# Attention decode block on one Trainium2 core: V as the moving operand, one V tile and wo loaded in parts, c and x as rows, the store from ACT

## The chip, the cores and the metric

The kernel runs on one core of one Trainium2 chip. The metric is device microseconds of one execution, as a median of several. Every experiment ran beside the kernel before on the same chip. A "ratio" is the mean time of one kernel's fast runs over that of the other's of the same rounds, so it is not quite the ratio of the medians that are quoted beside it. Profiles show one execution; its span is some 2 us shorter than the measured time (358.2 us beside 360.28 us for the kernel before).

## The reference, cut to what matters

One token goes through an adaptive-layernorm block: attention against a cache, then a small ReLU network. Everything is bf16.

```python
mod = (silu(c) @ w_mod)                     # six vectors of 512
h = layernorm(x) * (1 + ca) + sa
q = h @ wq                                  # 32 query heads of 128
# 8 kv heads, 4 query heads each, 32768 keys of 128: K and V are 64 MB each (2**20 bytes)
o = softmax(q k^T / sqrt(128)) v
x = x + ga * (o @ wo)                       # wo: 4096 x 512
h = layernorm(x) * (1 + cb) + sb
x = x + gb * (relu(h @ w1) @ w2)            # 512 -> 1792 -> 512
```

Nearly all of the 149.4 MB that must be read are K and V, and each is used once. The kernel is a stream of loads with computation beside it.

## The kernel before

All weights and tiles go through one ring of eight slots of 2 MB, in one order, from SP's queue. A tile of K or V is 128 partitions of 64 rows of 128 values: 16 KB per partition.

```python
stream = [("wm", 0), ("wm", 1), ("wq", 0), ("wq", 1)]
stream += [("k", 0, u) for u in range(NTILE)]
for g in range(Hkv):
    if g == Hkv - 1:
        stream.append(("wo", 0))
    for u in range(NTILE):
        if g + 1 < Hkv:
            stream.append(("k", g + 1, u))
        stream.append(("v", g, u))
stream += [("wo", 1), ("w1",)] + [("w2", i) for i in range(len(W2P))]
# in load(key): one transfer per tile
        i = nc.sync.dma_start(out=t[:], in_=src)

def pv(g, u):                               # V tile as weights, probabilities move: 64 small matmuls
    # ... cut
    for j in range(TK):
        c0 = (16 * G + j % 16) * 32 + REP * (s0 + j // 16)
        nc.tensor.matmul(oT_ps[:], lhsT=Vsb[:, j, :], rhs=PT_g[:, c0:c0 + REP],
                         start=(u == 0 and j == 0), stop=(u == NTILE - 1 and j == TK - 1))

# the end: wo's second half lands last of the attention weights, then w1, then w2 in three parts
project(1)                                  # 64 matmuls
# ... residual, layernorm, 56 matmuls with w1, relu
x1_rows = rows4(x1T[:], "x1_rows")          # 16 matmuls of one column: x1 as four rows
# ... 56 matmuls with w2 into ffn_ps, then two vector operations
nc.sync.dma_start(out=..., in_=o_bf...)     # the result
```

`c` and `x` are loaded by ACT's queue as 128 columns, in pieces of 8 bytes.

## Time and profile before

| kernel before | value |
|---|---|
| time, median of 3 runs | 360.28 us (359.99 to 360.31) |
| span of the profiled run | 358.2 us |
| mean granted TensorE clock | 0.77 |

The page's part 1 (busy time of each engine and its share of the span), part 2 (the span in 40 slices: TensorE clock, DMA share in tenths, GB/s), parts 3 and 4 (DMA queues with packets, MB and share; the chain of waits by engine), and from part 5 the group of matmuls with V:

```profile
PE 237.5 (66%) x3138; PEld 136.9 (38%) x3138; DVE 184.5 (52%) x207; ACT 27.0 (8%) x65; POOL 8.3 (2%) x13
...
PEclk9999996986597659876698659686968869665555
DMA  7999999999999999999999999999999999999993
GB/s 302 428 434 423 430 437 432 417 435 432 434 421 437 428 426 432 434 424 432 434 429 424 432 429 435 426 426 432 428 435 427 423 435 434 426 426 435 426 413 119
...
q8 instruction: 24, 0.39, 0.4%
q10 hardware_dynamic: 288, 0.00, 0.0%
...
DMA 77%; DVE 11%; PE 10%; issue 1%; ACT 0%; DVEq 0%
...
L374 PE MATMUL oT_ps<-PT_g,Vsb 128*128 128x4 bf16 x2048 | 56.6, 164 | 9.5 <-DMA Vsb<-in_A_v_cache_dram 5.1
```

The DMA engines are full in all slices but the first and the last, at about 430 GB/s. No compute engine is near its limit (PE, the busiest, is at 66%). 149.4 MB at 430 GB/s are 347 us, so the span can only shrink by a leaner stream or by shorter ends. The chain of waits agrees: 77% of it is DMA. Queue q8 holds the instruction fetches: 24 packets and 0.39 MB for PE's 6090 instructions. They move on the same engines as the data (section 9: after the first of them one of the sixteen landings of a transfer comes about 1.3 us behind the rest).

The tail, from the timeline (start, duration, engine, line, operation, count, and in brackets the idle time before it with its releaser):

```profile
345.75 2.29 PE L407 MATMUL attnT_ps<-o_sb,wo_sb 128*128 128x1 bf16 x64 [2.29 <-DMA wo_sb<-in_A_wo_dram]
...
350.58 1.63 PE L450 MATMUL hidT_ps<-h2T,w_sb 128*128 128x1 bf16 x56 [1.28 <-DVE h2T L207]
...
352.14 1.00 PE L240 MATMUL x_rows_ps<-ident_f,x1T 128*1 128x32 f32 x29
...
353.07 1.78 PE L465 MATMUL ffn_ps<-w_sb,hidT 128*1 128x128 bf16 x50
...
354.48 0.10 PEld L465 LDWEIGHTS <-hidT 128*1 128x1 bf16 x7 [0.19 <-issue]
354.91 0.29 DVE L471 TENSOR_TENSOR o_rows<-ffn_ps,gb_rows_sb 128x128 f32<-128x128 f32 x1 [1.28 <-PE ffn_ps L465]
...
355.56 0.66 SPq L474 DMA_DIRECT2D out_dram<-o_bf  x1
```

The last wo part lands at 345.7 us. Its matmuls take 2.3 us, then come a layernorm, the hidden layer (350.58), x1_rows (352.14) and the matmuls with w2, until 354.9. The last weight loads of w2, at 354.48, come just as the last part of w2 lands (issued at 330.9, 23.6 us to landing). So the compute chain and the stream end nearly together.

### The profile page before, as it was taken

How to read it: one execution, taken by the hardware profiler on the slowest of the kernel's cores; microseconds unless marked ns; L12 is line 12 of the kernel's file. 1: busy time of each engine (PE TensorE's matmuls, PEld its weight loads, DVE VectorE, ACT ScalarE, POOL GpSimd, SP SyncE). 2: the span in 40 equal slices, each digit the busy share in tenths (PEclk: the TensorE clock that was granted, in tenths of full speed). 3: DMA queues.
4: the chain of work that ended last, by engine and by line, in shares of the span. 5: the costliest groups of instructions: out<-in, count | busy, mean ns of one | idle time of the engine just before them, and what ended most of it. 6: DMA issues, size and time to landing. Idle time of an engine off the chain costs nothing.

```text
span 358.2 us, 6817 instructions
## 1 busy us (share of the span) xinstructions
PE 237.5 (66%) x3138; PEld 136.9 (38%) x3138; DVE 184.5 (52%) x207; ACT 27.0 (8%) x65; POOL 8.3 (2%) x13
## 2 busy tenths in 40 slices
PE   0547775857587839755777758883956576895454
PEld 0543333433254425423343425341523334445354
DVE  4419976552954465553954385456655394342012
ACT  1111022002000110002000200011000100003000
POOL 9000000000000000000000000000000000000000
PEclk9999996986597659876698659686968869665555
DMA  7999999999999999999999999999999999999993
GB/s 302 428 434 423 430 437 432 417 435 432 434 421 437 428 426 432 434 424 432 434 429 424 432 429 435 426 426 432 428 435 427 423 435 434 426 426 435 426 413 119
DMA packets 11492, 149.86 MB, mean 418 GB/s; under 512 B 1480, under 2 KB 1480, under 8 KB 2376
## 3 DMA queue, kind: packets, MB, share of 16 engines
q1 hardware_dynamic: 11176, 149.43, 98.0%
q8 instruction: 24, 0.39, 0.4%
q10 hardware_dynamic: 288, 0.00, 0.0%
q14 instruction: 4, 0.03, 0.0%
HBM read 149.42 MB, written 0.00 MB: 417 GB/s over the span
## 4 chain that ended last, share of the span: by engine, by line
DMA 77%; DVE 11%; PE 10%; issue 1%; ACT 0%; DVEq 0%
DMA Ksb<-in_A_k_cache_dram 67%; DVE KTt L309 9%; DMA wo_sb<-in_A_wo_dram 9%; PE S_ps L318 6%; PE oT_ps L374 1%; DMA xc_bf<-in_c_dram 1%; PE attnT_ps L407 1%; PE ffn_ps L465 0%; PE hidT_ps L450 0%; ACT P_g L351 0%; DVE PT_g L356 0%; PE x_rows_ps L240 0%; DVE S_g L324 0%; PE stat_ps_ln L189 0%; PE L_ps L361 0%
## 5 line engine op out<-in xcount | busy, mean ns | idle before, releaser
L318 PE MATMUL S_ps<-KTt,qbd 128*128 128x512 bf16 x512 | 159.1, 475 | 59.8 <-DVE KTt L309 58.9
L309 DVE STREAM_TRANSPOSE KTt<-Ksb 128x2048 f32<-128x2048 f32 x64 | 143.7, 2286 | 47.6 <-DMA Ksb<-in_A_k_cache_dram 47.6
L318 PEld LDWEIGHTS <-qbd 128*128 128x128 bf16 x512 | 59.3, 117 | 148.5 <-issue 117.8
L374 PE MATMUL oT_ps<-PT_g,Vsb 128*128 128x4 bf16 x2048 | 56.6, 164 | 9.5 <-DMA Vsb<-in_A_v_cache_dram 5.1
L374 PEld LDWEIGHTS <-Vsb 128*128 128x128 bf16 x2048 | 56.3, 97 | 16.8 <-DMA Vsb<-in_A_v_cache_dram 5.4
L324 DVE TENSOR_SCALAR_CACHE_REDUCE S_g<-S_ps 128x512 f32<-128x512 f32 x16 | 11.0, 687 | 50.8 <-PE S_ps L318 50.8
L289 ACT COPY qbd<-qrep_sb 32x128 bf16<-32x128 bf16 x32 | 9.4, 295 | 187.0 <-PE S_ps L318 185.8
L356 DVE STREAM_TRANSPOSE PT_g<-P_g 128x1024 bf16<-128x1024 bf16 x8 | 10.0, 1245 | 17.5 <-ACT P_g L351 17.5
L361 PE MATMUL L_ps<-Lexp,ones_f 128*128 128x4 f32 x16 | 4.5, 351 | 21.1 <-DVE Lexp L359 21.1
L361 PEld LDWEIGHTS L_ps<-Lexp,ones_f 128*128 128x128 f32 x16 | 4.0, 311 | 21.5 <-issue 21.5
L383 DVE TENSOR_TENSOR oT_sb<-oT_ps,Linv 128x4 bf16<-128x4 f32 x8 | 1.3, 162 | 20.4 <-PE oT_ps L374 20.4
L226 PE MATMUL modT_ps<-siluT,wm_sb 128*128 128x1 bf16 x96 | 3.5, 172 | 10.8 <-DVE siluT L218 10.6
L351 ACT ACTIVATE P_g<-S_g,nbias 128x1024 bf16<-128x1024 f32 x8 | 9.2, 1147 | 0.2
L348 ACT ACTIVATE nbias<-Mb_ps 128x1 f32<-128x1 f32 x8 | 1.4, 172 | 90.2 <-PE Mb_ps L346 90.2
L226 PEld LDWEIGHTS <-wm_sb 128*128 128x128 bf16 x96 | 3.4, 118 | 10.8 <-DMA wm_sb<-in_w_mod_dram 7.5
L267 PE MATMUL qT_ps<-hT,wq_sb 128*128 128x1 bf16 x128 | 3.7, 165 | 5.2 <-DVE hT L207 2.7
L346 PE MATMUL Mb_ps<-ident_f,Mexp 1*128 1x1 f32 x16 | 3.5, 284 | 5.5 <-DVE Mexp L341 5.5
L407 PE MATMUL attnT_ps<-o_sb,wo_sb 128*128 128x1 bf16 x128 | 4.6, 172 | 2.3 <-DMA wo_sb<-in_A_wo_dram 2.3
L174 DVE CAST cT<-xc_bf 128x4 f32<-128x4 bf16 x1 | 3.8, 3764 | 4.2 <-DMA xc_bf<-in_c_dram 4.2
L346 PEld LDWEIGHTS Mb_ps<-ident_f,Mexp 1*128 1x128 f32 x16 | 2.8, 217 | 7.4 <-DVE Mexp L341 7.0
L267 PEld LDWEIGHTS <-wq_sb 128*128 128x128 bf16 x128 | 3.6, 104 | 5.3 <-issue 2.8
L407 PEld LDWEIGHTS <-wo_sb 128*128 128x128 bf16 x128 | 4.6, 119 | 2.4 <-DMA wo_sb<-in_A_wo_dram 2.4
(83 smaller groups left out, 53.5 us busy)
## 6 DMA issues: line engine op xcount, KB each, us to landing
Ksb<-in_A_k_cache_dram SPq DMA_DIRECT2D x32, 2048.0 KB, 34.0
Vsb<-in_A_v_cache_dram SPq DMA_DIRECT2D x32, 2048.0 KB, 34.5
wq_sb<-in_A_wq_dram SPq DMA_DIRECT2D x2, 2048.0 KB, 19.6
wo_sb<-in_A_wo_dram SPq DMA_DIRECT2D x2, 2048.0 KB, 31.9
wm_sb<-in_w_mod_dram SPq DMA_DIRECT2D x2, 1536.0 KB, 8.1
w_sb<-in_B_w_dram SPq DMA_DIRECT2D x1, 1792.0 KB, 33.8
w_sb<-in_B_w_dram SPq DMA_DIRECT2D x1, 1024.0 KB, 30.4
w_sb<-in_B_w_dram SPq DMA_DIRECT2D x1, 512.0 KB, 24.6
```

The costliest lines, as they stand in the source:

```text
L226: nc.tensor.matmul(modT_ps[:, j * KT + ko:j * KT + ko + 1], lhsT=lhsT[:, ko, :], rhs=siluT[:, kt:kt + 1], start=(kt == 0), stop=(kt == KT ...
L267: nc.tensor.matmul(qT_ps[:, hq:hq + 1], lhsT=wq_sb[kt // 2][:, kt % 2, hq * Dh:(hq + 1) * Dh], rhs=hT[:, kt:kt + 1], start=(kt == 0), stop ...
L289: nc.scalar.copy(out=o, in_=i)
L309: nc.vector.transpose(out=KTt[:].bitcast(F32), in_=Ksb[:, 32 * half:32 * half + 32, :].rearrange("p j d -> p (j d)").bitcast(F32),)
L318: nc.tensor.matmul(S_ps[:], lhsT=qbd[g % 2][:, hp, s, :], rhs=KTv[:, 16 * sl:16 * sl + 16, h, :, par], start=(t4 == 0 and sl == 0 and hp = ...
L324: nc.vector.tensor_scalar(out=S_tiles[g][:, G, :], in0=S_ps[:], scalar1=1.0, scalar2=None, op0=ALU.mult, op1=ALU.max, accum_out=m_tiles[g] ...
L346: nc.tensor.matmul(Mb_ps[:], lhsT=Mexp[:], rhs=ident_f[0:1, 0:1], start=True, stop=True)
L351: nc.scalar.activation(out=P_g[:], in_=S_g[:].rearrange("p g f -> p (g f)"), func=ACT.Exp, bias=nbias[:], scale=scale, accum_out=l_g[:],)
L356: nc.vector.transpose(out=PT_g[:], in_=P_g[:])
L361: nc.tensor.matmul(L_ps[:], lhsT=ones_f[:], rhs=Lexp[:], start=True, stop=True)
L374: nc.tensor.matmul(oT_ps[:], lhsT=Vsb[:, j, :], rhs=PT_g[:, c0:c0 + REP], start=(u == 0 and j == 0), stop=(u == NTILE - 1 and j == TK - 1),)
L407: nc.tensor.matmul(attnT_ps[:, ko:ko + 1], lhsT=wo_sb[:, r, :].rearrange("p (m ko) -> p ko m", ko=KT)[:, ko, :], rhs=o2[:, r:r + 1], start ...
```

## The change

The change bundles several ideas: fewer and wider matmuls for V, less work behind the last loads, a leaner start, and the store from another queue. It also cuts one V tile, the first of kv head 2, into three transfers by partitions. The diff, cut to its core:

```diff
+    PARTS = {("v", 2, 0): [(0, P - 16), (P - 16, P - 8), (P - 8, P)]}
-        i = nc.sync.dma_start(out=t[:], in_=src)
+        for lo, hi in PARTS.get(key, [(0, P)]):
+            stream_dma(t[lo:hi], src[lo:hi])            # also on SP's queue
 ...
+    stream += [("v", LAST, u) for u in range(NTILE - 1)]
+    stream += [("wo", 0), ("wo", 1), ("v", LAST, NTILE - 1), ("wo", 2)]   # heads 0-3, 4-5, 6-7
+    stream += [("w1",)] + [("w2", i) for i in range(len(W2P))]
 ...
+    need(("wm", 0))
+    xc_row = const.tile([1, 2, D], BF16)                # c and x as rows, then turned by 8 tiny matmuls
+    stream_dma(xc_row[:, 0, :], c)
+    stream_dma(xc_row[:, 1, :], A_x[0])
 ...
 def pv(g, u):                                           # for g != LAST; LAST keeps V as weights
+        for j in range(16):
+            c0 = (16 * G + j) * 32 + REP * s0
+            nc.tensor.matmul(
+                o_tiles[g][:], lhsT=PT_g[:, c0:c0 + 16],
+                rhs=Vsb[:].rearrange("p (s j) d -> p s j d", j=16)[:, :, j, :],
+                start=(u == 0 and j == 0), stop=(u == NTILE - 1 and j == 15),
+            )
 ...                                                     # then an ACT copy and 4 f32 matmuls per head
 def rows4(src_T, name):                                 # x1 and gb as rows
+        nc.vector.tensor_tensor(out=spread_f..., op=ALU.mult)
+        for kt in range(KT):
+            nc.tensor.matmul(r_ps[:, kt, :], lhsT=spread_f[:, kt, :], rhs=rsel32[:], start=True, stop=True)
 ...
-    nc.sync.dma_start(
+    nc.scalar.dma_start(
         out=out[0, 0].rearrange("(i n) -> i n", i=KT),
```

PE's program shrinks from 6090 to 3427 instructions (counted in the programs).

More of the change, by code (lines that the diff above doesn't have):

```diff
@@ L45 @@
     NG = NTILE // 2
-    GH = 4
-    HH = GH * REP
-    CH = P // HH
-    RH = Dh // CH
-    NHALF = Hkv // GH
+    WOP = [(0, Hkv // 2), (Hkv // 2, Hkv // 4), (3 * Hkv // 4, Hkv // 4)]
+    LAST = Hkv - 1
     FB = 2
@@ L63, with wo_v @@
     wq_v = A_wq.rearrange("(p kt) n -> p kt n", p=P)
-    wo_v = A_wo.rearrange("(b p r) d -> b p r d", p=P, r=RH)
+    def wo_v(i):
+        g0, n = WOP[i]
+        return A_wo[g0 * REP * Dh:(g0 + n) * REP * Dh, :].rearrange("(p r) d -> p r d", p=P)
     w1_v = B_w1.rearrange("(p kt) f -> p kt f", p=P)
@@ L100, in load @@
         elif kind == "wo":
-            t = ring.tile([P, RH, D], BF16, tag="slot", name="wo_sb")
-            src = wo_v[key[1]]
+            t = ring.tile([P, WOP[key[1]][1] * REP, D], BF16, tag="slot", name="wo_sb")
+            src = wo_v(key[1])
         elif kind == "w1":
@@ L109, in load, with stream_dma @@
             src = w2_v[:, a0:a0 + n]
-        i = nc.sync.dma_start(out=t[:], in_=src)
+        for lo, hi in PARTS.get(key, [(0, P)]):
+            stream_dma(t[lo:hi], src[lo:hi])
+        loaded[key] = t
+    def stream_dma(dst, src):
+        i = nc.sync.dma_start(out=dst, in_=src)
         tc.stamp_issue_order_token(i.ins, "sp_stream")
-        loaded[key] = t
     stream = [("wm", 0), ("wm", 1), ("wq", 0), ("wq", 1)]
     stream += [("k", 0, u) for u in range(NTILE)]
-    for g in range(Hkv):
-        if g == Hkv - 1:
-            stream.append(("wo", 0))
+    for g in range(LAST):
         for u in range(NTILE):
-            if g + 1 < Hkv:
-                stream.append(("k", g + 1, u))
-            stream.append(("v", g, u))
-    stream += [("wo", 1), ("w1",)] + [("w2", i) for i in range(len(W2P))]
+            stream += [("k", g + 1, u), ("v", g, u)]
+    stream += [("v", LAST, u) for u in range(NTILE - 1)]
+    stream += [("wo", 0), ("wo", 1), ("v", LAST, NTILE - 1), ("wo", 2)]
+    stream += [("w1",)] + [("w2", i) for i in range(len(W2P))]
     pos = [0]
@@ L130, in need @@
         return loaded[key]
-    xc_bf = const.tile([P, 2, KT], BF16)
-    nc.scalar.dma_start(out=xc_bf[:, 0, :], in_=c[0].rearrange("(p kt) -> p kt", p=P))
-    nc.scalar.dma_start(out=xc_bf[:, 1, :], in_=A_x[0, 0].rearrange("(p kt) -> p kt", p=P))
+    need(("wm", 0))
+    xc_row = const.tile([1, 2, D], BF16)
+    stream_dma(xc_row[:, 0, :], c)
+    stream_dma(xc_row[:, 1, :], A_x[0])
+    need(("wm", 1))
     ident_bf = const.tile([P, P], BF16)
@@ L158 @@
     )
-    cmask = const.tile([P, CH], F32)
+    cmask, rsel = {}, {}
+    for n in sorted({n * REP for _, n in WOP}):
+        cmask[n] = const.tile([P, P // n], F32, name=f"cmask{n}")
+        nc.vector.tensor_reduce(
+            out=cmask[n][:], in_=ident_f[:].rearrange("p (c r) -> p c r", r=n), op=ALU.add, axis=AX.X,
+        )
+        rsel_f = const.tile([P, n], F32, name=f"rsel_f{n}")
+        nc.vector.tensor_reduce(
+            out=rsel_f[:], in_=ident_f[:].rearrange("p (c r) -> p r c", r=n), op=ALU.add, axis=AX.X,
+        )
+        rsel[n] = const.tile([P, n], BF16, name=f"rsel{n}")
+        nc.vector.tensor_copy(out=rsel[n][:], in_=rsel_f[:])
@@ L161 @@
+    cmask32 = const.tile([P, KT], F32)
     nc.vector.tensor_reduce(
-        out=cmask[:], in_=ident_f[:].rearrange("p (c r) -> p c r", r=RH), op=ALU.add, axis=AX.X,
+        out=cmask32[:], in_=ident_f[:].rearrange("p (c r) -> p c r", r=32), op=ALU.add, axis=AX.X,
     )
-    rsel_f = const.tile([P, RH], F32)
+    rsel32 = const.tile([P, 32], F32)
     nc.vector.tensor_reduce(
-        out=rsel_f[:], in_=ident_f[:].rearrange("p (c r) -> p r c", r=RH), op=ALU.add, axis=AX.X,
+        out=rsel32[:], in_=ident_f[:].rearrange("p (c r) -> p r c", r=32), op=ALU.add, axis=AX.X,
@@ L167 @@
     )
-    rsel = const.tile([P, RH], BF16)
-    nc.vector.tensor_copy(out=rsel[:], in_=rsel_f[:])
+    spread_f = const.tile([P, KT, P], F32)
+    nc.gpsimd.memset(spread_f[:], 0.0)
+    osel = const.tile([16, 4, REP], F32)
+    nc.vector.tensor_copy(out=osel[:], in_=ident_f[0:16, 0:16].rearrange("p (s q) -> p s q", q=REP))
     oT_sb = const.tile([P, Hq], BF16)
-    oA = [const.tile([P, HH, CH], BF16, name=f"oA{i}") for i in range(NHALF)]
-    cT = const.tile([P, KT], F32)
-    nc.vector.tensor_copy(out=cT[:], in_=xc_bf[:, 0, :])
@@ L175 @@
-    xT = const.tile([P, KT], F32)
-    nc.vector.tensor_copy(out=xT[:], in_=xc_bf[:, 1, :])
+    oA = [const.tile([P, n * REP, P // (n * REP)], BF16, name=f"oA{i}") for i, (_, n) in enumerate(WOP)]
+    xc_ps = small_ps([P, 2, KT], "xc_ps")
+    for i in range(2):
+        cols = xc_row[:, i, :].rearrange("o (p kt) -> o kt p", kt=KT)
+        for kt in range(KT):
+            nc.tensor.matmul(
+                xc_ps[:, i, kt:kt + 1], lhsT=cols[:, kt, :], rhs=ident_bf[0:1, 0:1], start=True, stop=True,
+            )
@@ L178 @@
+    xc = const.tile([P, 2, KT], F32)
+    nc.vector.tensor_copy(out=xc[:], in_=xc_ps[:])
+    cT, xT = xc[:, 0, :], xc[:, 1, :]
     attnT_ps = ps_acc.tile([P, KT], F32)
@@ L212 @@
     e_t = const.tile([P, KT], F32)
-    nc.scalar.activation(out=e_t[:], in_=cT[:], func=ACT.Exp, scale=-1.0)
+    nc.scalar.activation(out=e_t[:], in_=cT, func=ACT.Exp, scale=-1.0)
     nc.vector.tensor_scalar(out=e_t[:], in0=e_t[:], scalar1=1.0, scalar2=None, op0=ALU.add)
@@ L217 @@
     siluT = const.tile([P, KT], BF16)
-    nc.vector.tensor_tensor(out=siluT[:], in0=cT[:], in1=sig[:], op=ALU.mult)
+    nc.vector.tensor_tensor(out=siluT[:], in0=cT, in1=sig[:], op=ALU.mult)
     wm_sb = [need(("wm", 0)), need(("wm", 1))]
@@ L233, in rows4 @@
     def rows4(src_T, name):
-        r_ps = small_ps([P, P], f"{name}_ps")
-        nc.vector.memset(r_ps[:], 0.0)
-        for i in range(KT):
-            dst = r_ps[32 * i:32 * i + 1, :].rearrange("o (n kt) -> o kt n", kt=KT)
-            for kt in range(KT):
-                nc.tensor.matmul(
-                    dst[:, kt, :], lhsT=src_T[:, kt:kt + 1], rhs=ident_f[:, 32 * i:32 * i + 32],
-                    start=True, stop=True, skip_group_check=True,
-                )
-        r_sb = const.tile([P, P], F32, name=f"{name}_sb")
-        nc.vector.tensor_copy(out=r_sb[:], in_=r_ps[:])
-        return r_sb
+        nc.vector.tensor_tensor(
+            out=spread_f[:].rearrange("p kt (i z) -> p kt i z", z=32)[:, :, :, 0],
+            in0=src_T.unsqueeze(2).to_broadcast([P, KT, KT]),
+            in1=cmask32[:].unsqueeze(1).to_broadcast([P, KT, KT]), op=ALU.mult,
+        )
+        r_ps = small_ps([P, KT, 32], f"{name}_ps")
+        for kt in range(KT):
+            nc.tensor.matmul(r_ps[:, kt, :], lhsT=spread_f[:, kt, :], rhs=rsel32[:], start=True, stop=True)
+        r_sb = const.tile([P, 32, KT], F32, name=f"{name}_sb")
+        nc.vector.tensor_copy(out=r_sb[:], in_=r_ps[:].rearrange("p kt n -> p n kt"))
+        return r_sb[:].rearrange("p n kt -> p (n kt)")
     gb_rows = rows4(modT_sb[:, 5 * KT:6 * KT], "gb_rows")
@@ L251 @@
     stat1 = const.tile([P, 2], F32)
-    nc.vector.reduce_sum(out=stat1[:, 0:1], in_=xT[:], axis=AX.X)
+    nc.vector.reduce_sum(out=stat1[:, 0:1], in_=xT, axis=AX.X)
     nca = const.tile([P, KT], F32)
@@ L260 @@
     )
-    layernorm_T(xT[:], stat1, hT[:], modT_sb[:, 0:KT], nca[:], "ln1")
+    layernorm_T(xT, stat1, hT[:], modT_sb[:, 0:KT], nca[:], "ln1")
     wq_sb = [need(("wq", 0)), need(("wq", 1))]
@@ L366, in pv @@
     def pv(g, u):
-        if u == 0:
-            o_tiles[g] = ps_o.tile([P, REP], F32, tag="o", name="oT_ps")
-        oT_ps, PT_g = o_tiles[g], PT_tiles[g]
+        PT_g = PT_tiles[g]
         Vsb = need(("v", g, u))
         G, s0 = u // 2, 4 * (u % 2)
-        for j in range(TK):
-            c0 = (16 * G + j % 16) * 32 + REP * (s0 + j // 16)
+        if g == LAST:
+            if u == 0:
+                o_tiles[g] = ps_o.tile([P, REP], F32, tag="oT", name="oT_ps", bufs=1)
+            for j in range(TK):
+                c0 = (16 * G + j % 16) * 32 + REP * (s0 + j // 16)
+                nc.tensor.matmul(
+                    o_tiles[g][:], lhsT=Vsb[:, j, :], rhs=PT_g[:, c0:c0 + REP],
+                    start=(u == 0 and j == 0), stop=(u == NTILE - 1 and j == TK - 1),
+                )
+            return
@@ L374, in pv @@
+        if u == 0:
+            o_tiles[g] = ps_o.tile([16, 4 * Dh], F32, tag="o", name="o_ps")
+        for j in range(16):
+            c0 = (16 * G + j) * 32 + REP * s0
             nc.tensor.matmul(
-                oT_ps[:], lhsT=Vsb[:, j, :], rhs=PT_g[:, c0:c0 + REP],
-                start=(u == 0 and j == 0), stop=(u == NTILE - 1 and j == TK - 1),
-            )
+                o_tiles[g][:], lhsT=PT_g[:, c0:c0 + 16],
+                rhs=Vsb[:].rearrange("p (s j) d -> p s j d", j=16)[:, :, j, :],
+                start=(u == 0 and j == 0), stop=(u == NTILE - 1 and j == 15),
+            )
@@ L379, in normalise, with part_of @@
+    def part_of(g):
+        return [i for i, (g0, n) in enumerate(WOP) if g0 <= g < g0 + n][0]
     def normalise(g):
-        b, gl = divmod(g, GH)
+        oT_ps = o_tiles.pop(g)
+        if g != LAST:
+            X = spool.tile([16, 4 * Dh], F32, tag="X", name="X")
+            nc.scalar.copy(out=X[:], in_=oT_ps[:])
+            oT_ps = ps_o.tile([P, REP], F32, tag="oT", name="oT_ps", bufs=1)
+            for s in range(4):
+                nc.tensor.matmul(
+                    oT_ps[:], lhsT=X[:, s * Dh:(s + 1) * Dh], rhs=osel[:, s, :], start=(s == 0), stop=(s == 3),
+                )
+        i = part_of(g)
+        g0, n = WOP[i]
+        CH = P // (n * REP)
@@ L382, in normalise @@
         o_g = oT_sb[:, REP * g:REP * (g + 1)]
-        nc.vector.tensor_tensor(out=o_g, in0=o_tiles.pop(g)[:], in1=Linv_tiles.pop(g)[:], op=ALU.mult)
+        nc.vector.tensor_tensor(out=o_g, in0=oT_ps[:], in1=Linv_tiles.pop(g)[:], op=ALU.mult)
         nc.vector.tensor_tensor(
-            out=oA[b][:, REP * gl:REP * (gl + 1), :],
+            out=oA[i][:, REP * (g - g0):REP * (g - g0 + 1), :],
             in0=o_g.unsqueeze(2).to_broadcast([P, REP, CH]),
-            in1=cmask[:].unsqueeze(1).to_broadcast([P, REP, CH]), op=ALU.mult,
+            in1=cmask[n * REP][:].unsqueeze(1).to_broadcast([P, REP, CH]), op=ALU.mult,
@@ L388, in normalise, with spread @@
         )
     o2_tiles = {}
-    def spread(b):
-        o2_ps = small_ps([P, RH], "o2_ps")
+    def spread(i):
+        n = WOP[i][1] * REP
+        o2_ps = small_ps([P, n], "o2_ps")
         nc.tensor.matmul(
-            o2_ps[:], lhsT=oA[b][:].rearrange("p h c -> p (h c)"), rhs=rsel[:], start=True, stop=True,
+            o2_ps[:], lhsT=oA[i][:].rearrange("p h c -> p (h c)"), rhs=rsel[n][:], start=True, stop=True,
         )
-        o2 = spool.tile([P, RH], BF16, tag="o2_sb", name="o2_sb")
+        o2 = const.tile([P, n], BF16, name=f"o2_sb{i}")
@@ L399, in spread, with project @@
         nc.vector.tensor_copy(out=o2[:], in_=o2_ps[:])
-        o2_tiles[b] = o2
-    def project(b):
-        o2 = o2_tiles.pop(b)
-        wo_sb = need(("wo", b))
-        for r in range(RH):
+        o2_tiles[i] = o2
+    def project(i):
+        n = WOP[i][1] * REP
+        wo_sb = need(("wo", i))
+        for r in range(n):
             for ko in range(KT):
@@ L409, in project @@
                     lhsT=wo_sb[:, r, :].rearrange("p (m ko) -> p ko m", ko=KT)[:, ko, :],
-                    rhs=o2[:, r:r + 1], start=False, stop=(b == NHALF - 1 and r == RH - 1),
+                    rhs=o2_tiles[i][:, r:r + 1], start=False, stop=(i == len(WOP) - 1 and r == n - 1),
                     skip_group_check=True,
@@ L423 @@
                 scores(g + 1, u)
+            if g == LAST and u == NTILE - 1:
+                for i in range(len(WOP) - 1):
+                    project(i)
             pv(g, u)
@@ L428 @@
         normalise(g)
-        if g % GH == GH - 1:
-            spread(g // GH)
-        if g == Hkv - 2:
-            project(0)
-    project(1)
+        if g + 1 == sum(WOP[part_of(g)]):
+            spread(part_of(g))
+    project(len(WOP) - 1)
+    ffn_ps = ps_s.tile([P, 512], F32, tag="s", name="ffn_ps")[:, 0:P]
+    nc.vector.memset(ffn_ps, 0.0)
     stat2 = const.tile([P, 2], F32)
@@ L439 @@
     nc.vector.scalar_tensor_tensor(
-        out=x1T[:], in0=x1T[:], scalar=1.0, in1=xT[:], op0=ALU.mult, op1=ALU.add, accum_out=stat2[:, 0:1],
+        out=x1T[:], in0=x1T[:], scalar=1.0, in1=xT, op0=ALU.mult, op1=ALU.add, accum_out=stat2[:, 0:1],
     )
@@ L455 @@
     nc.scalar.activation(out=hidT[:], in_=hidT_ps[:], func=ACT.Relu)
-    x1_rows = rows4(x1T[:], "x1_rows")
-    ffn_ps = small_ps([P, P], "ffn_ps")
-    nc.vector.memset(ffn_ps[:], 0.0)
     for part, (base, n) in enumerate(W2P):
@@ L469 @@
                     )
+        if part == 0:
+            x1_rows = rows4(x1T[:], "x1_rows")
     o_rows = const.tile([P, P], F32)
-    nc.vector.tensor_tensor(out=o_rows[:], in0=ffn_ps[:], in1=gb_rows[:], op=ALU.mult)
+    nc.vector.tensor_tensor(out=o_rows[:], in0=ffn_ps, in1=gb_rows, op=ALU.mult)
     o_bf = const.tile([P, P], BF16)
-    nc.vector.tensor_tensor(out=o_bf[:], in0=o_rows[:], in1=x1_rows[:], op=ALU.add)
-    nc.sync.dma_start(
+    nc.vector.tensor_tensor(out=o_bf[:], in0=o_rows[:], in1=x1_rows, op=ALU.add)
+    nc.scalar.dma_start(
         out=out[0, 0].rearrange("(i n) -> i n", i=KT),
```

## The prediction

> **What bounds the kernel before.** The load stream. The page's 40 slices show the 16 DMA engines 90% busy or more from the second slice to the last but one, at 412 to 437 GB/s. 149.4 MB at the steady 430 GB/s is 348 us of the 358.2 us span. PE (66%), DVE (52%) and ACT (8%) follow. Only three things can shorten the span: a leaner stream, a better balanced end, a shorter tail.
>
> **The tail before** (timeline after 340 us): last wo lands 345.7, its 64 matmuls take 2.3, layernorm 2.5; w1 lands 350.06, hidden layer 350.58 to 352.2, x1_rows to 353.1, ffn ends 354.9, store issued 355.56, end 358.2. The last w2 part lands at about 354.5, so compute and stream end together. From 350 to 354 us DMA runs at only 0.4 to 0.6 of its share: half of the engines finish some 4 us before the others.
>
> **What the change does.**
> 1. V as the moving operand for seven heads: 64 small matmuls per tile (1.75 us) become 16 of 512 columns. S matmuls of that width take about 0.22 us at full and 0.43 us at half clock, so 3.5 us per tile, 7 if throttled; some 28 us per head for scores and PV together at full clock, plus a softmax gap of 5 to 6 us, against 38.9 us of stream per head. There is room unless the clock stays at 0.5. [...] its clock steps last 3.4 us or multiples and reach 1.0 in busy stretches. I expect a mean clock of 0.8 to 0.95. Gain on the critical path: none directly. PE's program shrinks from 6090 to 3427 instructions, which removes part of the 0.39 MB of instruction fetches from the same DMA engines: estimate 0.3 us.
> 2. c and x as rows: 256 writes of 8 bytes leave the start. The first activation is not critical: 0 to 0.3 us.
> 3. One V tile in 112+8+8 partitions: [...]
> 4. wo in three parts: only 32 matmuls (1.15 us) stay behind the last wo. But w1's landing then binds the hidden layer, so about 0.5 us of this counts.
> 5. x1_rows now has four f32 weight loads of 128x128 (0.5 us each) instead of 32 short records: 2.0 us instead of 0.93, in front of ffn in PE's order. Loss about 1 us in the tail.
> 6. Store from ACT: 0 to 0.2 us gain.
>
> **Sum.** Stream end about 1.1 us earlier; tail about 0.5 us longer. Predicted 359.4 us, 8 in 10: 357.9 to 360.9. Faster by over 2%: 0.04; within 2%: 0.90; slower by over 2%: 0.06.
>
> **What would show it.** Slices: DMA still full, PE clock higher. Queues: instruction bytes down by 0.1 to 0.2 MB. Last w2 landing near 353.4. Timeline: x1_rows 2 us, delaying ffn.
>
> **What would make it wrong.** PE stays at half clock and becomes the bound (several per cent slower); engine balance goes the other way; x1_rows hidden by pulled-ahead weight loads (faster).

In step 1, the clock's steps are those of the trace of the kernel before (3.41, 6.83, 10.24 us and longer, at 0.5 or 1.0; 1.00 from 84.9 to 86.5 us, for one, where PE is busy throughout). The step 3 term: 0.6 us of gain at the end of the stream, or a loss of that size, the time of one 16 KB packet (0.611 us in this trace). The sum counts that term as a gain: it came to 359.4 us with it, and to 360.0 us without.

## More of the kernel before

The stream around the middle, by stretches of 4 us. The columns are the stretch, its length, busy time (and number of instructions) of PE, PE's weight loads, DVE, ACT and POOL, then the clock, the DMA share and GB/s:

```profile
120.00:124.00 4.00, 4.00 (x61) 2.27 (x60) 0.85 (x3) 1.06 (x4) 0.00 (x0) 0.77 1.00 426
...
128.00:132.00 4.00, 0.56 (x3) 0.53 (x4) 3.26 (x5) 0.00 (x0) 0.00 (x0) 0.50 1.00 430
```

## The result, and the profile after

The changed kernel takes 365.36 us (365.12 to 366.39, 4 runs), the kernel before 360.24 us beside it (359.99 to 360.31, 4 runs). The ratio is 1.0149, with a 95% interval of 1.0128 to 1.0169. It is slower, by 5 us or 1.5%. That is still within the 2% that the prediction thought most likely, but the time lies outside its range of 357.9 to 360.9 us.

The same parts of the page, after:

```profile
PE 277.5 (76%) x1811; PEld 129.9 (36%) x1811; DVE 189.4 (52%) x213; ACT 31.0 (9%) x72; POOL 8.8 (2%) x14
...
PEclk9999996999899869999899878997899989996555
DMA  8999999999999999999999999999999999999994
GB/s 313 434 428 431 429 429 428 431 433 431 424 433 433 339 197 428 431 431 428 430 431 428 429 429 431 433 433 431 433 433 427 431 433 431 426 426 433 424 419 163
...
q8 instruction: 14, 0.23, 0.2%
...
q10 hardware_dynamic: 8, 0.00, 0.0%
...
DMA 73%; PE 12%; DVE 10%; issue 3%; ACT 1%; POOL 0%; DVEq 0%; SPq 0%; POOLq 0%
...
L416 PE MATMUL o_ps<-Vsb,PT_g 128*16 128x512 bf16 x448 | 104.0, 386 | 3.8 <-DVE PT_g L385 3.3
```

Most of it is as predicted. The clock is higher (0.89 on average), the V matmuls have gone from 2048 to 448 of this kind, and the instruction bytes have dropped to 0.23 MB. But the row of GB/s has a hole, 339 and 197, in slices 14 and 15. The row of DMA shares shows nothing there: the engines count as busy. This is how to tell a starved stream from a slow one. A starved stream has a low share (in section 9's first attempt the slices with 92 and 3 GB/s have 0.2 and 0.0); here the share is full and the bytes are missing, so each packet takes longer.

The same stretches of 4 us, after:

```profile
120.00:124.00 4.00, 4.00 (x18) 1.50 (x17) 0.85 (x3) 1.18 (x4) 0.00 (x0) 0.90 1.07 365
124.00:128.00 4.00, 2.91 (x18) 1.79 (x17) 1.27 (x5) 1.13 (x3) 0.00 (x0) 0.96 1.02 258
128.00:132.00 4.00, 2.15 (x6) 0.76 (x6) 4.00 (x4) 0.86 (x2) 0.00 (x0) 0.50 1.13 147
132.00:136.00 4.00, 3.87 (x14) 1.63 (x12) 1.32 (x2) 0.00 (x0) 0.00 (x0) 0.69 0.82 205
136.00:140.00 4.00, 3.61 (x16) 1.47 (x17) 0.00 (x0) 0.00 (x0) 0.00 (x0) 1.00 1.01 430
```

Between 120 and 136 us, 3.9 MB are moved, where 430 GB/s would have moved 6.88 MB; at that rate the missing 2.98 MB are 6.9 us. Up to the V tile of kv head 2 the stream has 51 MB, which it reaches near 122 us: the hole is where the tile in three parts is loaded. Packets of 16 KB that take 0.611 us elsewhere take about 1.03 us from 123 to 127 us, and about 2.5 us from 130 to 132 us (medians of the trace's packet records; here and below a packet is counted by its start, from the start of the span).

The tail, after:

```profile
355.05 1.65 PE L511 MATMUL hidT_ps<-h2T,w_sb 128*128 128x1 bf16 x56 [1.46 <-DMA w_sb<-in_B_w_dram]
...
356.56 1.90 PE L272 MATMUL x_rows_ps<-rsel,spread_f 128*128 128x32 f32 x8
...
358.38 1.66 PE L523 MATMUL ffn_ps<-w_sb,hidT 128*1 128x128 bf16 x56
...
360.10 0.29 DVE L531 TENSOR_TENSOR o_rows<-ffn_ps,gb_rows_sb 128x128 f32<-128x128 f32 x1 [1.31 <-PE ffn_ps L523]
...
360.74 1.10 ACTq L534 DMA_DIRECT2D out_dram<-o_bf  x1
```

Here the predicted loss is seen as well: x1_rows stands in front of the w2 matmuls for 1.8 us (356.56 to 358.38), where it took about 0.9 before.

### The profile page after: what moved, and what is told of

Same layout as the page of the kernel before. It is cut to its first block, busy times and chain, and to the rows that moved or that the text cites. A ratio compares the mean times of both kernels' runs of the same rounds, so it can differ in the third digit from the quotient of the medians.

```text
span 363.2 us, 4176 instructions
## 1 busy us (share of the span) xinstructions
PE 277.5 (76%) x1811; PEld 129.9 (36%) x1811; DVE 189.4 (52%) x213; ACT 31.0 (9%) x72; POOL 8.8 (2%) x14
## 4 chain that ended last, share of the span: by engine, by line
DMA 73%; PE 12%; DVE 10%; issue 3%; ACT 1%; POOL 0%; DVEq 0%; SPq 0%; POOLq 0%
DMA Ksb<-in_A_k_cache_dram 65%; DMA w_sb<-in_B_w_dram 8%; DVE KTt L338 6%; PE o_ps L416 6%; PE S_ps L347 4%; DVE sel L158 2%; PE modT_ps L256 1%; DVE PT_g L385 1%; PE x_rows_ps L272 0%; PE hidT_ps L511 0%; PE ffn_ps L523 0%; ACT L380 0%; ACT P_g L380 0%; PE oT_ps L433 0%; DVE S_g L353 0%
## 5 line engine op out<-in xcount | busy, mean ns | idle before, releaser
L347 PE MATMUL S_ps<-KTt,qbd 128*128 128x512 bf16 x512 | 136.2, 414 | 46.3 <-DVE KTt L338 45.4
L416 PE MATMUL o_ps<-Vsb,PT_g 128*16 128x512 bf16 x448 | 104.0, 386 | 3.8 <-DVE PT_g L385 3.3
L347 PEld LDWEIGHTS <-qbd 128*128 128x128 bf16 x512 | 51.8, 104 | 121.1 <-issue 76.3
L416 PEld LDWEIGHTS <-PT_g 128*16 128x16 bf16 x448 | 38.5, 91 | 66.8 <-issue 15.1
L406 PE MATMUL oT_ps<-PT_g,Vsb 128*128 128x4 bf16 x256 | 7.6, 166 | 8.2 <-DMA Vsb<-in_A_v_cache_dram 4.4
L430 ACT COPY X<-o_ps 16x512 f32<-16x512 f32 x7 | 4.0, 575 | 83.4 <-PE o_ps L416 83.4
L406 PEld LDWEIGHTS <-Vsb 128*128 128x128 bf16 x256 | 7.5, 105 | 8.5 <-DMA Vsb<-in_A_v_cache_dram 4.5
L433 PE MATMUL oT_ps<-osel,X 16*128 16x4 f32 x56 | 7.4, 250 | 3.2 <-ACT X L430 3.2
L158 DVE COPY sel<-ident_bf 128x128 bf16<-128x128 bf16 x4 | 8.3, 4061 | 0.6 <-POOL ident_bf masks.py:199 0.6
L433 PEld LDWEIGHTS oT_ps<-osel,X 16*128 16x128 f32 x56 | 6.7, 186 | 4.6 <-ACT X L430 4.6
```

What stands on the lines that cost most here:

```text
L158: nc.vector.tensor_copy(out=sel[:, hp, :].rearrange("p (a c) -> p a c", a=4), in_=src)
L347: nc.tensor.matmul(S_ps[:], lhsT=qbd[g % 2][:, hp, s, :], rhs=KTv[:, 16 * sl:16 * sl + 16, h, :, par], start=(t4 == 0 and sl == 0 and hp = ...
L406: nc.tensor.matmul(o_tiles[g][:], lhsT=Vsb[:, j, :], rhs=PT_g[:, c0:c0 + REP], start=(u == 0 and j == 0), stop=(u == NTILE - 1 and j == TK ...
L416: nc.tensor.matmul(o_tiles[g][:], lhsT=PT_g[:, c0:c0 + 16], rhs=Vsb[:].rearrange("p (s j) d -> p s j d", j=16)[:, :, j, :], start=(u == 0 ...
L433: nc.tensor.matmul(oT_ps[:], lhsT=X[:, s * Dh:(s + 1) * Dh], rhs=osel[:, s, :], start=(s == 0), stop=(s == 3),)
```

## The experiments

Theory A: the cut by partitions changes which partitions are written at the same time; that makes each packet take longer and slows the stream itself. Rival B: V as the moving operand holds ring slots too long and the stream starves. Rival C: the cut costs because it makes more and smaller transfers, whatever its direction.

### 1. The change without the cut

```diff
-    PARTS = {("v", 2, 0): [(0, P - 16), (P - 16, P - 8), (P - 8, P)]}
+    PARTS = {}
```

> The changed kernel with the one V tile loaded in one transfer again, everything else as changed. Theory A (the split by partitions into 112+8+8 [...] so the stream itself slows): the stretch of 147 to 365 GB/s between 121 and 136 us is gone, time 359 to 361 us, so 4 to 6 us less than the changed kernel. Theory B (V as moving operand keeps PE busy, ring slots come free late, and the stream starves): still about 365 us, still a slow stretch.

Measured: 358.69 us (358.62 to 358.77) against 360.17 us for the kernel before, ratio 0.9959 (0.9944 to 0.9974). The stretches of 4 us of this run:

```profile
124.00:128.00 4.00, 1.79 (x13) 1.36 (x12) 2.39 (x5) 1.99 (x4) 0.00 (x0) 1.00 1.02 438
128.00:132.00 4.00, 3.27 (x10) 1.49 (x10) 4.00 (x4) 0.00 (x0) 0.00 (x0) 0.57 0.98 418
```

The hole is gone, and with it rival B. The rest of the change is worth 1.5 us. Later, beside other runs, the same kernel was timed again:

> The changed kernel without the split once more, for comparison on the same chip: 358.7 us within 0.3.

Measured: 358.52 us (358.50 to 358.80), ratio 0.9957. The cut costs the changed kernel 1.0149 / 0.9959 = 1.019 of its time, 6.8 us.

### 2. The kernel before with the cut alone

```diff
-        i = nc.sync.dma_start(out=t[:], in_=src)
+        for cut in ([(slice(0, 112),), (slice(112, 120),), (slice(120, 128),)] if key == ("v", 2, 0) else [()]):
+            i = nc.sync.dma_start(out=t[cut] if cut else t[:], in_=src[cut] if cut else src)
```

> The kernel before, with only this V tile loaded in 112+8+8 partitions. Theory A: 364 to 367 us, a slow stretch near 121 to 136 us, with 16 KB packets of about 1 us and then 2 to 2.5 us instead of 0.61. Theory B: 360.3 us, no slow stretch.

Measured: 367.52 us (366.85 to 368.81), ratio 1.0198 (1.0181 to 1.0215). One stretch of it:

```profile
128.00:132.00 4.00, 1.21 (x4) 0.78 (x5) 3.26 (x5) 0.00 (x0) 0.00 (x0) 0.50 1.11 188
```

The cut costs 7.3 us in the other kernel too. That is a little more than theory A's range. The packets are slow as expected: medians of 1.15 us from 123 to 127 us, then 1.91 us from 130 to 132 us.

### 3. The same cut along the free dimension

```diff
+ three transfers of 128 partitions each: rows 0-55, 56-59, 60-63 of every partition
```

> The kernel before, with this V tile loaded in three transfers of 128 partitions each, cut along the free dimension in the same ratio (56, 4 and 4 of 64 rows per partition). Theory A: 360.3 us within 0.4[...]. Rival C (three issues or small transfers cost it, whatever the direction of the cut): several us slower, as with the cut by partitions.

Measured: 360.08 us (359.96 to 360.42), ratio 0.9999 (0.9984 to 1.0014).

```profile
124.00:128.00 4.00, 0.49 (x3) 0.44 (x3) 1.76 (x5) 1.41 (x3) 0.00 (x0) 0.84 1.00 416
128.00:132.00 4.00, 1.53 (x5) 0.78 (x6) 3.52 (x3) 0.00 (x0) 0.00 (x0) 0.50 1.07 450
```

Three transfers of the same sizes cost nothing if each covers all 128 partitions. Rival C is out.

### 4. 112 and 16 partitions

> The kernel before, with this V tile in 112+16 partitions. If the 112-partition transfer[...] is itself slow, its packets take about 1 us again (7 x 0.4 us lost) and the 16-row transfer about 2.4 us[...] (1.8 lost): 363 to 366 us. If only the 8-partition transfers hurt: at most 361 us.

(The 7 is 112 packets over the page's 16 engines. The changed kernel's 112-partition transfer left sixteen landing records, from 129.3 to 135.2 us. The losses are my estimates from that kernel's packets of about 1.0 and 2.4 us.)

Measured: 366.64 us (366.12 to 366.95), ratio 1.0178; packets of 1.15 us (median) from 123 to 127 us. So the 112-partition transfer is slow by itself, and the two 8-partition transfers are not all of the loss. The 16-partition transfer was milder than expected: a median of 1.53 us for the packets from 130 to 132 us and none over 2.0, not 2.4. (The records do not say which packet belongs to which transfer.)

### 5. Eight partitions at a time: neighbours, or every fourth

In the trace of the changed kernel the 112-partition transfer and those of all 128 partitions leave sixteen landing records each, and the two 8-partition transfers eight each (132.0 to 134.9 us and 134.3 to 136.2 us). If I read a landing as one engine's, as in section 9, an 8-partition transfer runs on eight engines. Two kernels load the whole tile in such transfers, and differ only in which eight partitions a transfer covers: neighbours, or every fourth of a block of 32.

```diff
+ 16 transfers, partitions 8*i ... 8*i+7                    (neighbours)
+ 16 transfers, partitions 32*(i//4) + i%4, then every 4th   (steps)
```

> The kernel before, with this one V tile loaded in sixteen transfers of eight neighbouring partitions each. [...] 39 us in place of 4.9: 380 to 395 us. If only the number of engines matters (eight in place of sixteen): packets of 0.61 us, at most 366 us.

> The same sixteen transfers of eight partitions, but each takes every fourth partition of a block of 32[...]. Same bytes, same number of transfers, same engines. [...] packets mostly 0.61 us[...]; 360 to 367 us, so at least 15 us less than with neighbouring partitions. If the split as such (eight engines, many transfers) costs it: the same time as with neighbouring partitions.

In both, the first alternative is theory A's. The 39 us are sixteen transfers at an estimated 2.4 us a packet; the packets of the changed kernel took 2.47 us (median) from 130 to 132 us.

Measured: 375.02 us with neighbours (two runs, ratio 1.0413), 366.12 us with steps (four runs, ratio 1.0166). Same bytes, same number of transfers, same number of engines, 8.9 us apart. One stretch of each:

```profile
124.00:128.00 4.00, 0.46 (x3) 0.29 (x2) 1.99 (x6) 1.41 (x3) 0.00 (x0) 0.94 0.53 127
```

```profile
124.00:128.00 4.00, 0.41 (x3) 0.29 (x2) 1.99 (x6) 1.41 (x3) 0.00 (x0) 0.92 0.52 209
```

The DMA share is only 0.53 and 0.52: about half of the sixteen engines work at a time. The expected size for neighbours was too large: 375 us instead of 380 to 395, since the packets took 1.0 to 1.2 us and later 1.6 us, not 2.4. With steps the difference from neighbours was 8.9 us, not the 15 us that I had asked for. The steps still cost 5.9 us. Most of that is the half of the engines that stands idle: by an estimate from the 430 GB/s elsewhere and the 209 GB/s of this stretch, 2.1 MB at about half the rate take 4.9 us longer.

### 6. Which side decides

The last pair changed two things, since with the partitions it also changed which rows of HBM are read together. Two more kernels, with two runs each, change one side each. Rows land in other partitions than their probabilities expect, so their results are wrong. (They still passed the comparison, presumably because one permuted tile among 32 of V moves the result by less than its tolerance.)

> The sixteen transfers of eight partitions again, wrong on purpose: each writes eight neighbouring partitions, but reads every fourth row of a block of 32 in HBM. [...] as with neighbouring partitions before, packets of about 1 us, then 1.5 us, 374 to 376 us. If the HBM addresses decide: packets of 0.61 us for the first half, 365 to 367 us.

> The other way round, wrong on purpose: each transfer writes every fourth partition and reads eight neighbouring rows in HBM. [...] packets of 0.61 us in the first half, 365 to 367 us. If the HBM addresses decide: about 1 us, then 1.5 us, 374 to 376 us.

Medians of the 16 KB packets, counted from the traces' packet records, with the times of all runs of this kind:

```
writes to       reads from      us, median   packets that start in 123-127 us
neighbours      neighbours      375.02       1.13 us
neighbours      every fourth    375.34       1.29 us
every fourth    neighbours      366.53       0.611 us
every fourth    every fourth    366.12       0.611 us
```

The destination decides (1.13 and 1.29 us for neighbours, 0.611 us for every fourth, whichever rows are read), the HBM addresses do not. That the cause lies in which partitions are written at the same time is shown; why neighbours are slow is not. (No other step was tried.) A step of four restores 0.611 us in the first half of the tile only. In the second half (partitions 64 to 127) even the stepped packets slow down to 1.1 to 1.2 us at 132 us, and most packets of the 112-partition transfer took 1.0 to 1.2 us. Neither is explained, and the sizes remain open.

### 7. Where the 1.5 us of the rest come from

Four runs start from the change without the cut and undo one part each.

```diff
+ (7)  V as weights for all eight heads, as before
+ (8)  c and x as columns from ACT's queue, as before
+ (9)  x1_rows by 16 small matmuls, as before, still after the hidden layer
+ (10) the same, ahead of the hidden layer, where PE waits for w1
```

> The changed kernel without the split, and with V as weights for all eight heads, as before. If V as the moving operand gave part of the 1.5 us that the kernel without the split is ahead of the kernel before (through fewer instruction fetches on the same DMA engines): instruction bytes back to about 0.39 MB, and 0.3 to 0.8 us slower than without the split, 359.0 to 359.5. If it gave nothing: 358.7.

> The changed kernel without the split, and with c and x as columns from ACT's ring, as before. In the kernel without the split the first data packet starts about 0.6 us earlier than in the kernel before. If the columns' 256 small writes cause that: the first packet is 0.6 us later again and the time 359.0 to 359.4. If not: 358.7.

> The changed kernel without the split, with x1_rows made by the 16 small matmuls of before, at the same place (after the hidden layer). The prediction's term: 0.93 us in place of 1.76 us between hidden layer and ffn. If the tail is bound by compute there: 0.6 to 0.9 us faster, 357.8 to 358.1. If the last w2 load binds instead: under 0.3 us.

> As the last, but x1_rows is put ahead of the hidden layer, in the 1.4 us that PE waits there for w1. Then nothing stands between hidden layer and ffn but the relu: ffn starts about 1.4 us earlier than without the split; the last w2 load should bind: 357.2 to 357.9 us, faster than both kernels of the case.

Measured, with 360.23 us for the kernel before:

| run | us, median | ratio to before (95% interval) |
|---|---|---|
| 7: V as weights | 359.98 | 0.9993 (0.9981 to 1.0006) |
| 8: c and x as columns | 359.06 | 0.9965 (0.9953 to 0.9978) |
| 9: old x1_rows, same place | 358.48 | 0.9952 (0.9939 to 0.9964) |
| 10: old x1_rows, before w1 | 358.41 | 0.9950 (0.9937 to 0.9964) |

V as the moving operand gives 1.3 us of the 1.5. The rows for c and x give 0.2 to 0.3 us at most, which the intervals do not separate from nothing. The first data packet started 1.74 us after the start of the span both in run 8 and without the cut (1.95 us in the kernel before), so the explanation that I expected is not borne out.

Putting the old x1_rows back gains 0.2 us by the medians, not 0.8, and the intervals do not separate even that from nothing. The timelines show why. Without the cut, compute binds:

```profile
348.56 1.65 PE L511 MATMUL hidT_ps<-h2T,w_sb 128*128 128x1 bf16 x56 [1.42 <-DMA w_sb<-in_B_w_dram]
...
350.07 1.90 PE L272 MATMUL x_rows_ps<-rsel,spread_f 128*128 128x32 f32 x8
...
351.89 1.66 PE L523 MATMUL ffn_ps<-w_sb,hidT 128*1 128x128 bf16 x56
...
353.61 0.29 DVE L531 TENSOR_TENSOR o_rows<-ffn_ps,gb_rows_sb 128x128 f32<-128x128 f32 x1 [1.31 <-PE ffn_ps L523]
```

In run 10 nothing stands between hidden layer and w2 matmuls, but now these wait for w2 in two places:

```profile
348.78 1.63 PE L527 MATMUL hidT_ps<-h2T,w_sb 128*128 128x1 bf16 x56 [0.71 <-DVE h2T L237]
...
350.94 1.02 PE L539 MATMUL ffn_ps<-w_sb,hidT 128*1 128x128 bf16 x32 [0.53 <-DMA w_sb<-in_B_w_dram]
...
352.27 1.00 PE L539 MATMUL ffn_ps<-w_sb,hidT 128*1 128x128 bf16 x24 [0.31 <-DMA w_sb<-in_B_w_dram]
...
352.90 0.10 PEld L539 LDWEIGHTS <-hidT 128*1 128x1 bf16 x7 [0.22 <-issue]
353.33 0.29 DVE L545 TENSOR_TENSOR o_rows<-ffn_ps,gb_rows_sb 128x128 f32<-128x128 f32 x1 [4.60 <-PE ffn_ps L539]
```

The last operation starts 0.28 us earlier (353.33 against 353.61). So x1_rows cost 1 us of PE time, but only a quarter of it was ahead of the last load. Run 10 is the fastest of all, faster than both kernels; it cannot be told from run 9.

### 8. V as the moving operand alone, in the kernel before

> The kernel before with one part of the change alone: V as the moving operand for the first seven heads. If that part gives nearly all of the gain: instruction bytes about 0.23 MB, stream end 1.3 to 2 us earlier; but the compute tail of before, which still has 64 matmuls behind the last wo, keeps part of it: 358.8 to 359.6 us. If the parts only gain together: 360.0 to 360.3 us.

Measured: 358.87 us (358.55 to 359.11) against 360.24 us, ratio 0.9959 (0.9947 to 0.9972). This one part alone gives what the whole change gives without the cut.

### 9. Why it helps: the instruction fetches

The first attempt put three dummy matmuls behind each V matmul, to bring PE's program back to its old length.

> The changed kernel without the split, with three one-column dummy matmuls after each of the 448 V matmuls, into columns that nobody reads: V still moves, but PE's program has 6115 instructions again (3427 without them, 6090 in the kernel before). If V as the moving operand gains its 1.3 us through fewer instruction fetches on the DMA engines: instruction bytes back near 0.39 MB, the last data packet about 2 us later, 359.5 to 360.3 us. If it gains through something else (how PE reads V, the clock): 358.5 to 358.9 us. PE's extra work, about 28 x 48 x 0.027 = 36 us estimated from the small V matmuls of before, should stay under the stream; if PE turns into the bound, well over 361 us.

Measured: 380.48 us, a failed experiment. The dummies depended on nothing, so they were ordered ahead of real work: in the timeline 128 of them run in one piece at 51.03 us, before most of the matmuls with wq, at 63.67 us. The rows of DMA share and GB/s show the stream starved in slices 6 and 7, from 47 to 66 us.

```profile
DMA  8999920799999999999999999999999999999993
GB/s 313 433 427 426 429 92 3 312 431 427 386 398 429 433 427 436 424 436 427 433 429 428 434 424 437 422 438 427 431 434 426 435 422 438 427 431 433 426 414 149
```

The second attempt makes each dummy read its own V tile and probabilities.

> As the attempt with dummy matmuls, but each dummy reads the V tile and the probabilities of its own matmul, so that none can run ahead. PE's program has 6115 instructions, V still moves. If fewer instruction fetches are what V as the moving operand gains: instruction bytes 0.39 MB spread over the whole span, no stretch without DMA, 359.6 to 360.3 us. If the gain is something else: 358.5 to 359.0 us. If PE becomes the bound through its extra work: slices with DMA under 90%, and more than 361 us.

Measured: 366.28 us (363.68 to 367.50), ratio 1.0151. PE did become the bound, which the time alone could not tell from a cost of fetches. From this run's page, the row of GB/s, the fetches and the chain of waits by engine:

```profile
GB/s 309 436 430 430 432 431 428 432 430 428 432 430 432 430 432 428 424 432 428 429 430 426 432 429 430 430 428 432 432 430 429 432 430 432 428 430 429 420 243 0
...
q8 instruction: 24, 0.39, 0.4%
...
PE 77%; DVE 10%; DMA 8%; ACT 2%; issue 1%; POOL 0%; DVEq 0%; POOLq 0%
```

But its stream ran without a gap until 340 us, so the stream itself can be compared. Counted from the packet records, data moved from 20 to 300 us, and the landing of the last part of w2:

| run | V | fetches | GB/s | last landing, us |
|---|---|---|---|---|
| kernel before | weights | 24 | 428.7 | 354.4 |
| cut along the free dimension (section 3) | weights | 24 | 428.4 | 354.7 |
| without the cut, V as weights (section 7, run 7) | weights | 24 | 428.8 | 354.3 |
| dummies that read V (section 9, second attempt) | moving | 24 | 428.7 | 354.4 |
| without the cut (section 1) | moving | 14 | 430.1 | 352.9 |
| kernel before, V moving (section 8) | moving | 14 | 429.9 | 353.2 |

Both the rate and the end of the stream follow the number of fetches, not the operand. From 20 to 300 us the kernel without the cut moved 0.39 MB more than the kernel before, and fetched only 0.15 MB less.

Why a fetch costs more than its bytes can be read from the landings. A transfer over all 128 partitions leaves sixteen landing records, as many as there are DMA engines; I read them as one for each engine. In the kernel before, those of the transfer that ends at 15.9 us lie within 0.6 us. After the first fetch (18.7 us) one engine lags about 1.3 us behind the rest, after two fetches two engines lag, after eight fetches eight. The ninth fetch (146.5 us) puts one engine a second step behind, the seventeenth (270.1 us) a third. So each fetch delays one engine by 1.2 to 1.4 us, and the pattern is that of fetches going in turn to eight of the sixteen engines. At the last landing seven engines are three steps behind and end at 354.0 to 354.4 us, while seven others were done by 350.6 us. With 14 fetches no engine is more than two steps behind, and the last ends at 352.9 us. The slowest engine ends the stream, so the third step is about the gain of 1.3 us. (A few 8 KB packets of queue q14 add smaller lags.) The packet of a fetch takes 0.93 us in the records, one of data 0.61 us; why it delays its engine by more than that is open.

## Why the prediction was wrong

- What bounds the kernel: right. DMA is 77% of the chain of waits before and 73% after, and PE, busy for 76% of the span, did not bind.
- Step 1, V moving: right in kind, mis-sized. 16 matmuls take 3.55 us per tile (estimate 3.5), the mean clock is 0.89 (0.8 to 0.95), the instruction bytes fell by 0.16 MB (0.1 to 0.2). The gain was estimated as 0.3 us from bytes alone, as if all sixteen engines shared them; alone it measured 1.4 us, and 1.3 us when undone, since the slowest engine has two fetches to carry in place of three.
- Step 2, c and x as rows: 0.2 to 0.3 us, within the estimate and within noise.
- Step 3, the tile in three parts (the term was 0.6 us of gain at the end, or a loss of that size): this is the step that failed. It took for granted that each packet still takes 0.61 us, and did not ask where the packets are written. Packets took 1.03 us and then 2.47 us in the place of the 0.61 us. The cut cost 6.8 us here and 7.3 us in the kernel before. A run of the cut alone, as in section 2, would have shown it. The uneven engines that the cut was meant to balance are mostly the work of the instruction fetches (section 9).
- Step 4, wo in parts: PE did wait for w1 (1.4 us without the cut), as predicted. What this part gives by itself was not tried.
- Step 5, x1_rows: 1.76 us in the chain as against 2.0 predicted; but it cost the kernel 0.2 us at most, not 1, since the last w2 load waits close behind.
- Step 6, the store from ACT: nothing seen. From the last vector operation to the end of the span it is 2.69 us before and 2.68 us without the cut (end of o_bf to end of span).
- Without the failed step the sum would have been 360.0 us; 358.69 was measured. The fetches (1.0 us more than estimated) and x1_rows (0.8 us less) cover that difference and a little more.
- "What would make it wrong" named the engine balance, as a loss of 0.6 us; it did not name slower packets.

## What to carry to other kernels

Do not cut a transfer by partitions to balance DMA engines: every such cut tried here cost 5.9 us or more, even the one by steps. Cut along the free dimension, which cost nothing here (ratio 0.9999). When GB/s drops under a full DMA share, look at the time per packet (here 0.611 us, and 2.47 us in the hole), not at waits. In a kernel bound by its loads, a shorter instruction program can be worth more than its bytes (here 1.3 us for 0.16 MB, by an estimate 0.4 us at 430 GB/s): look at how late the slowest DMA engine lands. A part that is cheap to undo should be run alone before it is bundled with others.
